# A hand-ordered attention and gated-MLP kernel on one core: new orders for all five engines, and a planner that counts instruction packets and load landings differently

## The chip, the cores and the metric

The kernel runs on one core of one Trainium2 chip. The time is that of one execution on the device, in microseconds. Three runs of the kernel before the change took 268.81, 270.65 and 270.70 us; their median is 270.65 us. One more execution, taken with the hardware profiler, took 270.25 us; its span, from the first instruction of the program to the last event that the profile sees, is 268.5 us. All durations below come from that one execution, and its time axis starts with the span.

## The reference, cut to what matters

S is 2048 tokens, D is 512, there are 32 heads of 16 elements, and the hidden size of the gated MLP is 1792. The 2048 tokens are cut into N = 4 segments of L = 512 tokens.

```python
x = A_x
g = sigmoid((x * gate_w).sum(-1, keepdims=True))
# part A: attention inside each segment, plus a memory of all segments before it
q, k, v = x @ wq, x @ wk, x @ wv            # per head, per segment of 512 tokens
for s in range(4):
    logits = qs @ ks.T * 0.25 + causal_mask
    a_dot  = softmax(logits) @ vs
    a_mem  = (phi(qs) @ M) / (phi(qs) @ z + 1e-6)    # phi(t) = t+1 if t>0 else exp(t)
    o      = sigmoid(beta) * a_mem + (1 - sigmoid(beta)) * a_dot
    M, z   = M + phi(ks).T @ vs, z + phi(ks).sum(0)
a = concat(o) @ wo
# part B
b = (gelu(x @ w_gate) * (x @ w_up)) @ w_down
out = g * a + (1 - g) * b
```

All inputs and the output are bfloat16; sums are kept in float32.

## The kernel before

**Tasks.** The work is cut into 1215 named tasks. A task runs on one engine and holds one or a few instructions. Names carry the segment first. `K1_2.0` and `K1_2.2` are the two halves (two matmuls each, over the four 128-row blocks of D) of tile 2 of K of segment 1; `Q`, `V`, `G` (gate), `U` (up) and `D` (down and wo) are named alike. `G1_10` is gate tile 10 of 14 for segment 1. In segment 0, K is cut into eight matmuls of 256 columns a tile (`K0_0.0` to `K0_0.7`), and Q goes to the four X banks. `warm0` to `warm10` multiply constants at the start, `x0t...` transpose x of segment 0 on TensorE and `x0ev...` copy it out. `Kn_tev`, `Qn_tev`, `Vevn_t` and `Gevn_t` copy a tile out of PSUM on ScalarE or VectorE; `Um` multiplies an up tile with the gelu of its gate tile; `kp`, `kl` write masked copies of K. `gmul`, `gsum`, `gexs`, `gts` make the output gate; `gmul0` needs `gate_w` broadcast (`w_gwb`).

**Attention.** For each group t of heads there are four or five rounds `qk s_t A0, B0, (L), A1, B1` (lines 849 to 905): matmuls into the four X banks, one exp on ScalarE over 2048 columns (L866), and a causal mask on GpSimd (L869). The next round must wait until exp has read the X banks. Between two rounds TensorE gets plain matmuls, mostly ten. `pv s_t_j` (L908, L916) multiplies the probabilities with V; `pvt` and `norm` follow on VectorE.

**Memory.** `pke s_i` (exp of K, ScalarE) and `pkc s_i` (three instructions on VectorE, L690, L692, L694) make phi(K) in place, i being the half of K's tiles. `pkT s_t` transposes tile t of it into `phkt` by DMA (L824, issued through L524). `mz s` (L828) multiplies it with V, and `num` reads the memory for the next segment. `xt s` later loads x into the same buffer `phkt`, and so waits for `mz` of the segment before. `Vlo s_j` (L744) copies half of V's rows into another layout, also by DMA, once all four V tiles are copied out.

**Loads.** wk and wq are issued by ScalarE's queue, everything else by SP's, in the order of SP's list, through `wdma` (L537) and `xdma` (L542), both over L528 or L524. The gate weights come in two halves: `w_wg0` holds tiles 0 to 6, `w_wg1` tiles 7 to 13 (L577). The up and down weights (`w_wu0`, `w_wu1`, `w_wd0`, `w_wd1`) come in halves too and are held back by reading a "tick" that an exp of segment 0 writes.

**What sets the order.** `ORDER` (line 36) is a list of task names for each engine, and each engine executes its list in that order. `schedule` (L235) doesn't choose an order. It walks the five lists with estimated durations and so fixes which of the four PSUM banks W a group of matmuls takes: the one that its estimates find free first. It also models DMA: a load lands at `dma_free`, which grows with the bytes and `DMA_RATE`. And it models the fetch of TensorE's instructions in blocks of `BLOCK`, each asked for when `BLOCK_ASK` instructions of it are done and needed at `BLOCK_END`. `Emitter.plan` and `finalize` then put a semaphore wait on every instruction whose operands another engine or a DMA writes, so the lists change what waits for what, not what is computed. SP also works strictly in its list's order: while it waits for one task's operands, no later load is issued.

```python
            best = None
            for e in ENGINES:
                t = queue[e][-1]          # the next task of this engine's list
                if npred[t.id]:
                    continue
...
            if t.nbytes:
                dma_free = max(t.finish + DMA_LAT, dma_free) + t.nbytes / DMA_RATE
                avail = dma_free
```

Of the kernel before, what the change touches and what calls it, by code (L numbers as in the profile page):

```python
# [7 lines left out]
PE, ACT, DVE, POOL, SP = "pe", "act", "dve", "pool", "sp"  # L8
# [26 lines left out]
BLOCK, BLOCK_ASK, BLOCK_END = 256, 165, 208  # L35
# [4 lines left out]
        "K0_1.4 K0_1.5 K0_1.6 K0_1.7 K0_0.4 K0_0.5 K0_0.6 K0_0.7 K0_3.3 K0_2.4 K0_2.5 K0_2.6 K0_3.4 K0_3.5 Q0_2.0 "  # L40
        "Q0_1.0 Q0_1.2 Q0_2.2 Q0_3.0 K0_2.7 Q0_3.2 K0_3.6 Q0_0.0 Q0_0.2 K0_3.7 V0_1.0 V0_1.2 V0_0.0 V0_0.2 "
        "qk0_0A0 G0_5.0 G0_5.2 V0_3.0 V0_2.0 V0_2.2 qk0_0B0 V0_3.2 Q1_3.0 Q1_3.2 G1_10.0 G1_10.2 qk0_0L G0_1.0 "
        "G0_1.2 G0_9.0 G0_9.2 G0_7.0 qk0_0A1 G1_9.0 Q1_0.0 G0_4.0 G1_9.2 G0_4.2 qk0_0B1 G0_7.2 G1_7.0 G1_7.2 "
        "Q1_0.2 G1_1.0 G1_1.2 qk0_1A0 G1_11.0 G1_5.0 G1_5.2 G1_11.2 Q1_1.0 qk0_1B0 G0_6.0 G1_2.0 Q1_1.2 G0_10.0 "
        "G1_2.2 qk0_1A1 G0_6.2 K1_2.0 G0_10.2 pv0_0_1 pv0_0_0 qk0_1B1 K1_2.2 K1_1.0 G1_8.0 Q1_2.0 Q1_2.2 qk0_2A0 "
        "G1_8.2 K1_1.2 G0_8.0 G0_8.2 G0_3.0 qk0_2B0 V1_2.0 G0_3.2 V1_2.2 pv0_1_1 pv0_1_0 qk0_2L mz0 V1_0.0 "
        "G0_13.0 V1_0.2 qk0_2A1 G0_13.2 V1_3.0 G1_12.0 V1_3.2 G0_2.0 qk0_2B1 G1_12.2 G1_0.0 G0_2.2 G1_0.2 G0_0.0 "
        "G0_0.2 qk0_3A0 K1_0.0 G1_6.0 G1_6.2 K1_0.2 G0_12.0 qk0_3B0 K1_3.0 G0_12.2 K1_3.2 Q2_2.0 Q2_2.2 qk0_3A1 "
        "G1_3.0 G1_3.2 G0_11.0 G0_11.2 pv0_2_1 pv0_2_0 qk0_3B1 V1_1.0 Q2_0.0 Q2_0.2 Q2_3.0 Q2_3.2 G1_13.0 V1_1.2 "
        "G1_4.0 G1_4.2 G1_13.2 U0_1.0 U0_1.2 U0_2.0 U0_4.0 U0_2.2 U0_9.0 U0_0.0 U0_4.2 U0_0.2 qk1_0A0 U0_9.2 "  # L50
        "U0_3.0 U0_3.2 U0_7.0 U0_7.2 U0_10.0 U0_8.0 U0_8.2 U0_13.0 U0_13.2 U1_0.0 U1_0.2 U0_5.0 U0_10.2 U0_5.2 "
        "U1_13.0 num1_00.0 U1_1.0 U1_1.2 U1_10.0 U1_13.2 U1_10.2 U0_6.0 U1_7.0 U0_6.2 U1_5.0 U1_7.2 U1_2.0 "
        "qk1_0B0 U1_5.2 U1_2.2 U1_11.0 pv0_3_0 pv0_3_1 qk1_0L U0_11.0 Q2_1.0 Q2_1.2 U1_3.0 U0_11.2 qk1_0A1 U1_3.2 "
        "D0_0.0 D0_0.2 num1_01.0 D0_0.4 U1_11.2 qk1_0B1 U0_12.0 num1_02.0 U0_12.2 D0_0.6 D0_0.8 D0_2.0 qk1_1A0 "
        "D0_0.10 U1_8.0 U1_6.0 U1_8.2 U1_6.2 D0_0.12 qk1_1B0 D0_0.14 D0_2.2 D0_0.16 D0_2.4 D0_2.6 qk1_1A1 D0_2.8 "
        "num1_12.0 num1_10.0 num1_11.0 D0_2.10 D0_2.12 D0_2.14 qk1_1B1 D0_2.16 U1_12.0 U1_9.0 U1_9.2 U1_12.2 "
        "qk1_2A0 pv1_0_0 pv1_0_1 pv1_1_1 mz1 pv1_1_0 qk1_2B0 D0_1.0 D0_1.2 D0_1.4 D0_1.6 D0_1.8 V2_3.0 qk1_2L "
        "D0_1.10 D0_1.12 D0_1.14 D0_1.16 V2_3.2 qk1_2A1 V2_0.0 D0_3.0 U1_4.0 K2_0.0 U1_4.2 qk1_2B1 V2_0.2 D0_3.2 "
        "K2_3.0 D0_3.4 K2_0.2 qk1_3A0 K2_3.2 K2_1.0 D0_3.6 K2_2.0 K2_1.2 qk1_3B0 K2_2.2 D0_3.8 V2_1.0 D0_3.10 "
        "D0_3.12 qk1_3A1 D0_3.14 D0_3.16 V2_1.2 Q3_1.0 Q3_1.2 G2_0.0 qk1_3B1 pv1_2_0 pv1_2_1 G2_0.2 G2_1.0 G2_3.0 "  # L60
        "G2_2.0 G2_3.2 G2_1.2 G2_2.2 G2_6.0 G2_6.2 G2_7.0 G2_4.0 G2_4.2 G2_5.0 G2_5.2 qk2_0A0 pv1_3_0 pv1_3_1 "
        "G2_7.2 G2_8.0 G2_10.0 G2_8.2 G2_10.2 G2_9.0 G2_9.2 G2_11.0 G2_12.0 G2_11.2 G2_12.2 G2_13.0 G2_13.2 "
        "U2_9.0 U2_9.2 num2_01.0 U2_8.0 U2_8.2 D1_0.0 D1_0.2 num2_00.0 D1_0.4 U2_13.0 U2_13.2 qk2_0B0 num2_02.0 "
# [36 lines left out]
    "dve": (  # L100
        "x0ev0a_0 x0ev0b_0 x0ev1_0 x0ev0_1 x0ev1_1 K0_1ev kl0_11 kp0_1 kl0_10 Q0_1ev K0_2ev kp0_2 Q0_0ev gmul0 "
        "gsum0_3 Vev0_0 Gev0_5 gsum0_0 kl0_31 kp0_0 gsum0_1 Q1_3ev Gev1_10 Vev0_3 gmat Gev0_9 pkc0_0 Gev1_9 kp0_3 "
        "Gev0_4 Gev1_7 Q1_0ev Gev0_7 Gev1_1 kl0_30 Gev1_5 Gev1_11 pkc0_1 Gev1_2 Gev0_6 Gev0_10 pvt0_0_1 pvt0_0_0 "
# [98 lines left out]
class Sched:  # L202
# [32 lines left out]
    def schedule(self):  # L235
# [8 lines left out]
        dma_free = 0.0  # L244
# [931 lines left out]
```

## Time and profile before

| what | value |
|---|---|
| median of three runs | 270.65 us |
| the profiled execution | 270.25 us |
| its span | 268.5 us |
| TensorE busy | 262.4 us (98%) |
| ScalarE busy | 210.5 us (78%) |
| VectorE busy | 202.2 us (75%) |
| GpSimd busy | 105.1 us (39%) |
| TensorE instruction packets (queue q8) | 23, 0.38 MB |
| granted TensorE clock | 1.00 |

In the lists of groups and in the timeline a line begins with start and length in microseconds (the timeline) or with the source line (the groups); then come engine, operation, output <- inputs, shapes and, after an x, how many alike were merged. `[0.44 <-DMA wq]` says that the engine was idle for 0.44 us just before, and that the DMA of wq ended it. PE is TensorE's matmul, PEld its weight load, DVE VectorE, ACT ScalarE, POOL GpSimd, SPq the DMA issues of SP's queue. A DMA line gives name, queue, count, size of one, and the median time from the beginning of its issue to its landing. The last matmul ends 2.9 us before the end of the span; the last copy and the last store to memory lie there.

### The profile page before, as it was taken

What the parts mean: (1) busy time and instruction counts of PE and PEld (TensorE: products, weight loads), DVE (VectorE), ACT (ScalarE), POOL (GpSimd) and SP (SyncE); (2) the same over time, 40 slices, a digit from 0 to 9 for tenths busy, and PEclk for the clock granted to TensorE, in tenths of its full rate; (3) what the DMA queues carried; (4) which work ended last, traced back from release to release, by engine and by line L of the source; (5) the groups of instructions that cost most, each with busy time, mean ns of one, the idle gap of its engine ahead of it and who ended that gap; (6) DMA issues with size and microseconds to landing.
All of it is one profiled execution on the core that took longest, in us unless ns stands there. A gap on an engine that the chain in (4) does not pass through costs nothing.

```text
span 268.5 us, 7155 instructions
## 1 busy us (share of the span) xinstructions
PE 262.4 (98%) x3021; PEld 119.2 (44%) x3021; DVE 202.2 (75%) x399; ACT 210.5 (78%) x180; POOL 105.1 (39%) x256
## 2 busy tenths in 40 slices
PE   8999999999999999899999999999999999999995
PEld 4543345334444435433444443543444444443452
DVE  1689989878988897868985877897691885685662
ACT  2689899989998987788868897779888768776801
POOL 8106582785200346161520628313771072326310
DMA  6950732892000055520000146230000002400002
GB/s 221 319 148 0 172 89 24 256 295 78 2 0 2 1 85 126 147 63 2 0 2 0 22 88 75 61 101 20 2 1 2 2 0 62 99 23 22 22 1 78
DMA packets 32752, 18.23 MB, mean 68 GB/s; under 512 B 20560, under 2 KB 32720, under 8 KB 32720
## 3 DMA queue, kind: packets, MB, share of 16 engines
q1 hardware_dynamic: 31632, 16.73, 25.6%
q10 hardware_dynamic: 1088, 1.05, 1.2%
q8 instruction: 23, 0.38, 0.6%
q14 instruction: 9, 0.07, 0.1%
HBM read 9.84 MB, written 2.10 MB: 44 GB/s over the span
## 4 chain that ended last, share of the span: by engine, by line
PE 90%; DMA 5%; SPq 2%; ACT 1%; issue 1%; ACTq 1%
PE psW L497 71%; PE psXALL L860 9%; PE psW L908 6%; DMA wq<-in_A_wq_dram 3%; PE psXALL L497 3%; DMA xT<-in_A_x_dram 2%; SPq L524 2%; PE psW L916 1%; ACT ptl L866 1%; ACTq L528 1%; PE psW L828 0%; SPq L528 0%; ACT ost L1036 0%; ACT hT L511 0%; ACTq L393 0%
## 5 line engine op out<-in xcount | busy, mean ns | idle before, releaser
L866 ACT ACTIVATE pt<-psXALL 128x2048 bf16<-128x2048 f32 x64 | 120.1, 1877 | 27.3 <-PE psXALL L860 24.5
L869 POOL TENSOR_SCALAR_AFFINE_SELECT pt<-pt 128x256 bf16<-128x256 bf16 x128 | 55.3, 443 | 111.9 <-ACT pt L866 107.0
L497 PE MATMUL psW<-xT,wu 128*128 128x512 bf16 x224 | 55.9, 380 | 0.0
L497 PE MATMUL psW<-wd,hT 128*128 128x512 bf16 x210 | 55.3, 380 | 0.0
L497 PE MATMUL psW<-xT,wg 128*128 128x512 bf16 x224 | 53.7, 380 | 0.0
L1007 DVE TENSOR_TENSOR hT<-psW,hT 128x512 bf16<-128x512 f32 x56 | 37.1, 684 | 19.1 <-PE psW L497 18.8
L869 POOL TENSOR_SCALAR_AFFINE_SELECT ptl<-ptl 128x512 bf16<-128x512 bf16 x32 | 23.9, 746 | 29.1 <-ACT ptl L866 27.4
L497 PEld LDWEIGHTS psW<-xT,wg 128*128 128x128 bf16 x224 | 20.6, 98 | 25.8 <-issue 1.9
L497 PEld LDWEIGHTS psW<-xT,wu 128*128 128x128 bf16 x224 | 20.7, 98 | 24.2 <-issue 1.7
L497 PEld LDWEIGHTS psW<-wd,hT 128*128 128x128 bf16 x210 | 18.4, 98 | 21.2 <-issue 2.7
L922 DVE STREAM_TRANSPOSE tb<-psW 128x512 f32<-128x512 f32 x32 | 21.7, 701 | 8.0 <-PE psW L916 7.7
L860 PE MATMUL psXALL<-qT,kpad 32*128 32x320 bf16 (+3 forms) x512 | 25.7, 273 | 1.3 <-issue 1.3
L860 PEld LDWEIGHTS psXALL<-qT,kpad 32*128 32x128 bf16 x512 | 7.7, 92 | 26.3 <-ACT pt L866 15.7
L908 PE MATMUL psW<-pt,vaug 128*17 128x192 bf16 (+3 forms) x512 | 18.8, 273 | 0.0
L991 ACT ACTIVATE hT<-psW 128x512 bf16<-128x512 f32 x28 | 15.3, 596 | 4.5 <-PE psW L497 4.5
L771 POOL COPY exsT<-exs 32x4 f32<-32x4 f32 x64 | 15.4, 240 | 8.2 <-ACT exs L762 4.6
L866 ACT ACTIVATE ptl<-psXALL 128x2048 bf16<-128x2048 f32 x8 | 15.0, 1877 | 4.5 <-PE psXALL L860 4.4
L497 PE MATMUL psW<-wv,xT 128*128 128x512 bf16 x64 | 18.1, 380 | 0.0
L497 PE MATMUL psW<-xT,wk 128*128 128x512 bf16 (+1 forms) x80 | 18.0, 337 | 0.0
L497 PE MATMUL psW<-wo,oT 128*128 128x512 bf16 x60 | 16.7, 379 | 0.1
L514 DVE CAST hT<-psW 128x512 bf16<-128x512 f32 x20 | 13.5, 686 | 4.3 <-PE psW L497 4.3
L908 PEld LDWEIGHTS psW<-pt,vaug 128*17 128x17 bf16 x512 | 10.4, 90 | 8.0 <-issue 3.0
(101 smaller groups left out, 310.7 us busy)
## 6 DMA issues: line engine op xcount, KB each, us to landing
out_dram<-ost SPq DMA_DIRECT2D x15, 128.0 KB, 2.0
wg<-in_B_w_gate_dram SPq DMA_DIRECT2D x2, 896.0 KB, 7.1
wu<-in_B_w_up_dram SPq DMA_DIRECT2D x2, 896.0 KB, 7.1
wd<-in_B_w_down_dram SPq DMA_DIRECT2D x2, 896.0 KB, 6.4
phkt<-in_A_x_dram SPq DMA_DIRECT2D x3, 512.0 KB, 5.1
vlow<-vaug SPq DMA_DIRECT2D x8, 136.0 KB, 2.7
wk<-in_A_wk_dram ACTq DMA_DIRECT2D x2, 256.0 KB, 4.6
hT<-in_A_x_dram SPq DMA_DIRECT2D x2, 256.0 KB, 4.2
```

Of the source, the lines that this page charges most:

```text
L497: return Instr(lambda e: e.matmul(view(), lhsT, rhs, start=first, stop=last), reads=reads, writes=[fkey if fkey is not None else g.key], e ...
L514: alts[DVE] = [Instr(lambda e: e.tensor_copy(dst(), src()), reads=reads, writes=writes, est=dve_t(n))]
L524: return e.dma_start_transpose(out_ap(), in_ap())
L528: return e.dma_start(out_ap(), in_ap())
L771: cross = task(f"exsT{s}", POOL, [Instr(lambda e, g=g, c=c: e.tensor_copy(exsT[sl][32 * g:32 * g + 32, c:16:4], exs[32 * c:32 * c + 32, s4 ...
L860: instrs.append(Instr(lambda e, g=g, lhs=lhs, rhs=rhs, c0=c0, ncol=ncol: e.matmul(X[g][:, c0:c0 + ncol], lhs(32 * g), rhs(32 * g), start=T ...
L866: exp_task(s, f"exp{s}_{t}{name}", [Instr(lambda e: e.activation(dst[:], XALL[:, :].rearrange("p (g c) -> p g c", g=4), ACTF.Exp, scale=AT ...
L869: task(f"msk{s}_{t}{name}", POOL, [Instr(lambda e, view=view, pat=pat, base=base: e.affine_select(out=view, in_=view, compare_op=ALU.is_ge ...
L908: instrs.append(Instr(lambda e, t=t, q=q, kb=kb, slot=slot, c0=c0: e.matmul(gp.f32()[32 * q:32 * q + 17, 128 * kb + 64:512], Vaug[sl][:, k ...
L922: task(f"pvt{s}_{t}_{j}", DVE, [Instr(lambda e: e.transpose(Tb[:, j, :], gp.f32()[:, :]), [gp.key], [("Tb", j)], dve_t(512))], grp=gp)
L991: lambda e, g=g, ft=ft, s=s: e.activation(hT[s % 2][:, ft, :], g.f32()[:, :], ACTF.Gelu_apprx_tanh),
L1007: task(f"Um{s}_{ft}", DVE, [Instr(lambda e, g=g, ft=ft: e.tensor_tensor(hT[sl][:, ft, :], g.f32()[:, :], hT[sl][:, ft, :], ALU.mult), [g.k ...
```

## The change

The five lists of `ORDER` are replaced by others. The planner's constants for the instruction fetch change; a table `LANDING` gives fixed landing times for the loads of the head, and in `schedule` a load that is in this table sets `dma_free` to its entry. Five byte counts in the planner are raised: xt from 524288 to 700000, wu and wd from 917504 to 1050000, wo from 524288 to 600000. No instruction is added or removed: each engine has the same tasks, except that some copies out of PSUM move between ScalarE and VectorE (three of the copies of x of segment 0 go from VectorE to ScalarE, all four `Vev0` now run on VectorE). The diff of the lists, cut to the places that are spoken of here:

```diff
-BLOCK, BLOCK_ASK, BLOCK_END = 256, 165, 208
+BLOCK, BLOCK_ASK, BLOCK_END = 254.4, 172, 192
+LANDING = {
+    "w_wk0": 4.8, "x0_0": 4.4, "w_wk1": 6.2, "x0_1": 5.8, "w_wq0": 8.2, "w_wv0": 7.4, "w_wq1": 10.1, "w_wv1": 8.9,
+    "w_wg0": 11.5, "x1_0": 12.1, "w_gwb": 12.4, "x1_1": 13.0, "w_beta": 13.3, "x1_2": 13.8, "x1_3": 14.3,
+    "w_wg1": 18.0,
+}
 ORDER = {
     "pe": (
...
-        "K0_1.4 K0_1.5 K0_1.6 K0_1.7 K0_0.4 K0_0.5 K0_0.6 K0_0.7 K0_3.3 K0_2.4 K0_2.5 K0_2.6 K0_3.4 K0_3.5 Q0_2.0 "
-        "Q0_1.0 Q0_1.2 Q0_2.2 Q0_3.0 K0_2.7 Q0_3.2 K0_3.6 Q0_0.0 Q0_0.2 K0_3.7 V0_1.0 V0_1.2 V0_0.0 V0_0.2 "
-        "qk0_0A0 G0_5.0 G0_5.2 V0_3.0 V0_2.0 V0_2.2 qk0_0B0 V0_3.2 Q1_3.0 Q1_3.2 G1_10.0 G1_10.2 qk0_0L G0_1.0 "
...
+        "K0_0.4 K0_0.5 K0_0.6 K0_3.3 K0_2.4 K0_0.7 K0_1.4 K0_3.4 K0_2.5 K0_2.6 K0_2.7 K0_1.5 K0_1.6 K0_1.7 K0_3.5 "
+        "Q0_0.0 Q0_1.0 K0_3.6 K0_3.7 Q0_0.2 Q0_1.2 Q0_2.0 Q0_3.0 Q0_3.2 Q0_2.2 V0_0.0 V0_0.2 V0_2.0 qk0_0A0 "
+        "V0_3.0 V0_1.0 V0_2.2 V0_3.2 V0_1.2 G0_5.0 qk0_0B0 G0_5.2 G0_1.0 G0_1.2 G1_5.0 G1_10.0 qk0_0L G1_10.2 "
...
-        "qk1_2A0 pv1_0_0 pv1_0_1 pv1_1_1 mz1 pv1_1_0 qk1_2B0 D0_1.0 D0_1.2 D0_1.4 D0_1.6 D0_1.8 V2_3.0 qk1_2L "
...
+        "D0_2.16 pv1_0_1 pv1_0_0 qk1_2A0 V2_3.0 D0_1.0 pv1_1_1 mz1 qk1_2B0 D0_1.2 D0_1.4 D0_1.6 D0_1.8 D0_1.10 "
+        "qk1_2L pv1_1_0 D0_1.12 D0_1.14 V2_3.2 U1_4.0 U1_4.2 qk1_2A1 D0_1.16 K2_3.0 D0_3.0 D0_3.2 D0_3.4 qk1_2B1 "
...
     "act": (
...
+        "w_wk0 w_wk1 w_wq0 w_wq1 tload x0ev0b_0 x0ev1_0 x0ev1_1 K0_0even K0_1ev K0_0ev pke0_0 Q0_1ev Q0_0ev "
+        "Q0_3ev Q0_2ev kl0_00 kl0_01 exp0_0A0 kl0_10 exp0_0B0 gsum0_3 exp0_0L gexp exp0_0A1 Gev1_9 exp0_0B1 "
...
     "dve": (
-        "x0ev0a_0 x0ev0b_0 x0ev1_0 x0ev0_1 x0ev1_1 K0_1ev kl0_11 kp0_1 kl0_10 Q0_1ev K0_2ev kp0_2 Q0_0ev gmul0 "
-        "gsum0_3 Vev0_0 Gev0_5 gsum0_0 kl0_31 kp0_0 gsum0_1 Q1_3ev Gev1_10 Vev0_3 gmat Gev0_9 pkc0_0 Gev1_9 kp0_3 "
...
+        "x0ev0a_0 x0ev0_1 K0_2ev kp0_2 kl0_11 K0_3ev kl0_30 gmul0 gsum0_2 kp0_1 kp0_0 kl0_20 Vev0_0 Vev0_2 Vev0_3 "
+        "Vev0_1 Gev0_5 Gev0_1 pkc0_0 kl0_31 Gev1_10 Gev0_9 Gev1_5 gmat gsum0_0 Q1_3ev Gev0_10 Q1_0ev gsum0_1 "
...
     "sp": (
-        "x0_0 x0_1 w_wv0 w_wv1 w_wg0 x1_0 w_gwb x1_1 w_beta x1_2 x1_3 w_wg1 pkT0_0 pkT0_1 Vlo0_0 Vlo0_1 w_wu0 "
-        "pkT0_3 pkT0_2 x2_3 xt1 w_wd0 w_wu1 x2_0 x2_2 x2_1 w_wd1 w_wo x3_1 oTd1_0 Vlo1_1 pkT1_0 Vlo1_0 oTd1_1 "
...
+        "x0_0 x0_1 w_wv0 w_wv1 w_wg0 x1_0 w_gwb x1_1 w_beta x1_2 x1_3 Vlo0_1 pkT0_1 w_wg1 Vlo0_0 pkT0_3 pkT0_2 "
+        "x2_3 pkT0_0 w_wd0 w_wu1 x2_1 x2_0 xt1 x2_2 w_wu0 w_wo Vlo1_1 w_wd1 oTd1_0 oTd1_1 pkT1_1 Vlo1_0 pkT1_0 "
...
@@ schedule @@
             if t.nbytes:
                 dma_free = max(t.finish + DMA_LAT, dma_free) + t.nbytes / DMA_RATE
+                if t.name in LANDING:
+                    dma_free = LANDING[t.name]
                 avail = dma_free
```

## The prediction

> **What bounds the kernel now.** I read the page's busy line first, then the chain of waits in order of time, then PE's timeline around each break of that chain, and last the timeline of the SP queue, the landing times of single DMAs and VectorE's timeline.
>
> ```profile
> PE 262.4 (98%) x3021; PEld 119.2 (44%) x3021; DVE 202.2 (75%) x399; ACT 210.5 (78%) x180; POOL 105.1 (39%) x256
> ...
> 10.50 1.47 PE L497 MATMUL psXALL<-xT,wq 128*128 128x512 bf16 x6 [0.44 <-DMA wq<-in_A_wq_dram]
> ...
> 57.52 0.38 PE L497 MATMUL psW<-xT,wq 128*128 128x512 bf16 x1
> 58.38 0.82 PE L497 MATMUL psW<-xT,wq 128*128 128x512 bf16 x3 [0.48 <-DMA xT<-in_A_x_dram]
> ...
> 108.83 0.31 PE L860 MATMUL psXALL<-qT,kpad 32*128 32x320 bf16 x3
> 110.42 0.39 PE L860 MATMUL psXALL<-qT,kpad 32*128 32x320 bf16 x5 [1.28 <-issue]
> ```
>
> TensorE is busy 98% of the span; no other engine is over 78%. So an order can gain only what TensorE loses in pauses, and a new pause costs its full length. A 512-column matmul starts 0.2165 us after the one before it (ten of them take 2.26 us in the chain, the last with a tail of about 0.16 us), so the pauses are read from starts. 57.52 to 58.38 is 0.86 instead of 0.22: 0.64 us lost on the landing of x of segment 2. 108.83 to 110.42 is 1.58 us lost ("issue": no semaphore is late; five attention and memory groups, 192 matmuls in 3.2 us, have outrun the instruction fetch). The same way, 0.60 us go before 10.50 (second half of wq), 0.31 us at 174.07 (six matmuls in 1.77 us instead of 1.46, after a like run of 192), and 0.20 us at 27.91. Together 3.3 us: that is all there is to win.
>
> **What the change takes away.** (1) Before the wq wait the new order puts all 32 K matmuls, where the old one had 29. Three more of 0.109 us are done by 10.49: -0.33 us; the rest of that wait stays. (2) In the old list w_wd0, w_wu1 and three x2 tiles stood behind xt1, which SP could issue only at 46.42, after mz0. In the new one w_wd0, w_wu1, x2_1 and x2_0 stand ahead of xt1 and can go from about 42, after exp0_2A0; xt1, x2_2 and w_wu0 follow mz0, which now comes at about 48.1. The old run moved 2.36 MB (xt1 and the two weight halves) from about 48.4 to 56.7, 0.284 MB/us; at that rate x2_2 has landed by about 54, and Q2_2.2 comes at 56.1: -0.64 us. w_wu0 then lands at about 57 and U0_1.0 comes at 59.1. (These times leave out any new pause, which would move both alike.) (3) The run pv1, pv1, pv1, mz1, pv1 is split: two groups, qk1_2A0 with two plain tasks, pv1_1_1 and mz1, then qk1_2B0 and ten plain matmuls, and only then pv1_1_0. 3021 matmuls were fetched in 23 instruction packets (the page's queue q8), 131 each. In the old trace the two dense runs went through 136 matmuls in 2.0 and 2.5 us and then paused; from 136 matmuls before the first stop (106.6) to the resumption at 110.42 it is 3.8 us, which I take as the time that a packet needs. Adding up the starts of the same kinds of matmuls in the new order, its densest 136 take 5.2 us: -1.58 and -0.31 us. (4) The 0.20 us at 27.91 goes, as that sequence is gone. Sum: **-3.1 us**, with 2.0 as the low end if one fetch or landing is late again. One more switch between plain and tiled matmuls (0.10 us in, 0.11 to 0.17 us out) adds **+0.2 us**. A lowered cost in the planner moves nothing by itself; only the four lists and the bank choices reach the chip.
>
> **What it moves that the timeline of SP prices.** In the SP list w_wg1, the second half of the gate weights, was directly behind x1_3; now it stands behind Vlo0_1 and pkT0_1.
>
> ```profile
> 5.09 0.57 SPq L528 DMA_DIRECT2D gwb<-in_gate_w_dram  x1
> ...
> 8.41 4.26 SPq L524 DMA_TRANSPOSE xT<-in_A_x_dram  x2
> 12.71 0.58 SPq L528 DMA_DIRECT2D wg<-in_B_w_gate_dram  x1
> 25.77 2.53 SPq L524 DMA_TRANSPOSE phkt<-kT  x2
> 28.42 1.36 SPq L528 DMA_DIRECT2D vlow<-vaug  x2
> 29.83 0.62 SPq L528 DMA_DIRECT2D wu<-in_B_w_up_dram  x1
> ```
>
> The reader is to see the gap from 12.71 to 25.77: SP issues in order, and the first phkt transpose had to wait for phi(K) on VectorE. w_wg1 was issued ahead of that gap; the new list puts it behind. Its landing in `LANDING` is a constant, 18.0, whatever the issue time.
>
> ```profile
> wg<-in_B_w_gate_dram SPq DMA_DIRECT2D x1, 896.0 KB, 5.2
> ...
> wu<-in_B_w_up_dram SPq DMA_DIRECT2D x1, 896.0 KB, 5.9
> ...
> gwb<-in_gate_w_dram SPq DMA_DIRECT2D x1, 128.0 KB, 7.7
> ...
> 23.32 0.59 DVE L690 TENSOR_SCALAR kT<-kT 128x1024 bf16<-128x1024 bf16 x1
> 23.83 0.87 DVE L692 TENSOR_SCALAR pex<-pex 128x1024 bf16<-128x1024 bf16 x1
> 24.73 1.01 DVE L694 TENSOR_TENSOR kT<-kT,pex 128x1024 bf16<-128x1024 bf16 x1
> ```
>
> When w_wg1 can be issued: in the new VectorE list pkc0_0 (the three rows above) stands behind gmul0, which needs gwb: 5.09 + 7.7 = 12.8. From there: gmul0 1.22, gsum0_2 0.65, three kp writes and kl0_20 about 0.9, four V copies at 0.61 from start to start, Gev0_5 0.61: 18.6. Gev0_1 waits for G0_1.2 on TensorE, done at about 19.3, and takes 0.65: 20.0. pkc0_0 took 2.42 us in the old trace and its sister pkc0_1 1.48: done at 21.5 to 22.4. Vlo0_1 has gone by then. pkT0_1 issues for 1.26 us (half of 2.53), so w_wg1 is issued at 22.8 to 23.7. The 896 KB landed 5.2 us after issue for wg and 5.9 for wu beside the V copies; here Vlo0_0 follows at once. So it lands at **27.9 to 29.6**, middle 28.7.
>
> When TensorE needs it: gate tile 10 is in that half, and G1_10.0 is the first to want it. In the new order, from the wq landing at 10.49 there are 38 plain matmuls (12 of Q, 16 of V, 10 of G) at 0.2165 and two qk groups at 0.43: 10.49 + 8.23 + 0.86 = **19.6**. The other guards on the way are met: the V copies free the banks from 17 on, Q's copies free X at about 14.0. The wait is 8.4 to 10.0 us, and I take **+9.2**. Behind G1_10.0 on TensorE stands everything, qk0_0L first, so ScalarE starves as well; SP, GpSimd and VectorE do not depend on it before pkT0_1, so it ends by itself. In the old order the same tile was asked for at 19.47 and had landed at 17.9: 1.6 us of slack were there. Nothing later gives the 9.2 us back, since TensorE has no idle time left to fill.
>
> What the pause does to the pace: in the old trace the 1.28 us pause at 109.14 was followed by matmuls at full pace: 0. The other row is the head, where a TensorE that had done nothing needs 4.07 us for ten warm-up matmuls (4,864 columns, 2.06 us at full pace, plus the tail): 1.8 us lost. A pause of nine microseconds is seven times the longest one seen, so I side with the head row: **+1.8**, with 0 as the other end. [...]
>
> **Sum.** The profiled run took 270.25 us for its span of 268.5; it lies 0.4 under the median of 270.65. 270.25 - 3.1 + 0.2 + 9.2 + 1.8 = **278.3 us**.
>
> **Rivals.**
> - The wait, without the slow pace (the 109.14 row holds for nine microseconds too): 276.5 us. Chance 0.14.
> - The wait and a second one: w_wu0 is now issued at about 51, last of the loads, and U0_1.0 comes at 59.1. One wu load landed in 5.9 us, but the median of the two is 7.1, so the other took 8.3; then U0_1.0 is up to 0.3 us late, and if a packet comes late as well, 1.58 stays: 278.3 + 1.9 = 280.2 us. Chance 0.13.
> - The other side, w_wg1 is not late. If SP reached it before 19.6 - 5.2 = 14.4 us, all pauses but half of the wq one would go and nothing come: 270.25 - 3.1 + 0.2 = 267.3 us, faster by over 1%. For it speaks that the old trace has SP free from 13.3 on; against it that pkT0_1 reads what pkc0_0 writes. It decides at one place, the end of pkc0_0. Chance 0.03.
> - The change does little: TensorE waits 3 us at most at G1_10.0 and stays at full pace, so gain and loss cancel: up to 270.4 us. That needs w_wg1 issued by 17.4, so pkc0_0 done by 16, ahead of the V copies that precede it. Chance 0.02.
> - The forecast: 0.68.
>
> **Numbers.** The range takes the low wait without the slow pace (270.25 - 2.9 + 8.4 = 275.8) and the long wait with one gain lost (270.25 - 1.8 + 10.0 + 1.8 = 280.3). The runs of before spread over 0.7%, so 1% is about what can be told from no change. Faster by over 1%: 0.03; within: 0.02; slower: 0.95.
>
> **What the new profile would show.** PE's timeline: one gap of 8 to 10 us before a matmul on wg at about 19.5, its releaser the DMA of wg, issued at about 23; then some 4 us in which 512-column matmuls start 0.43 apart. No "issue" gap near 100 to 110, no wait on xT near 60 to 70. The end is as now, with the last matmul 2.9 us before the end of the span. Wrong would be: wg issued before 15, or a gap that another tile had filled.

## The result, and the profile after

The changed kernel takes **283.29 us** (median of six runs), the kernel before 270.67 us (median of six runs beside them): a ratio of 1.0458, 95% interval 1.0404 to 1.0513. Medians here and below are of all executions, while ratios leave out those in a second, slower state (of the changed kernel's six one, 288.04 us; the other five have a median of 282.78). The forecast was 278.3 us with a range up to 280.3. The direction and the place of the main loss were right; the time lies 5.0 us above the forecast and 3.0 us above the range (4.5 and 2.5 by the median of the five). The profiled execution took 283.8 us (before: 270.25) for a span of 281.4 us (before: 268.5). What stood at L497 stands at L504 now, and all lines below it are 7 further down likewise; in some of the experiments they shift by one to three more, since a list is wrapped anew or a task is added.

The page's first two parts, engines and slices (PEclk is the granted TensorE clock in tenths, in 40 slices of 7.0 us):

```profile
PE 258.8 (92%) x2981; PEld 119.1 (42%) x3021; DVE 203.3 (72%) x400; ACT 208.0 (74%) x179; POOL 104.5 (37%) x256
...
PEclk9995799999999999999999999999999999999999
```

TensorE was busy 98% of the span and is busy 92%; the other engines do what they did. 40 of its 3021 matmul records are missing from this trace, so small gaps of 0.16 us in its timeline mean nothing; where small losses count, I add up the starts of the weight loads, which are all there. TensorE's timeline shows where the time went, in three breaks:

```profile
17.77 1.67 PE L504 MATMUL psW<-xT,wg 128*128 128x512 bf16 x7 [0.16 <-DVE vaug L521]
28.19 1.03 PE L504 MATMUL psW<-xT,wg 128*128 128x512 bf16 x2 [8.74 <-DMA wg<-in_B_w_gate_dram]
...
125.26 0.59 PE L504 MATMUL psW<-xT,wk 128*128 128x512 bf16 x2
129.30 1.04 PE L504 MATMUL psW<-wo,oT 128*128 128x512 bf16 x4 [3.44 <-DVE hT L1014]
...
187.35 0.29 PE L923 MATMUL psW<-ptl,vlow 128*17 128x64 bf16 x16
189.47 0.38 PE L504 MATMUL psW<-wv,xT 128*128 128x512 bf16 x1 [1.83 <-DVE tb L929]
```

The first break is the predicted one, in front of G1_10.0. The other two were not predicted: VectorE releases TensorE late in front of D0_3.0 (129.30) and V3_2.0 (189.47). The chain of waits tells why. Around the first break (start, length, what):

```profile
21.43 0.29 DVE klow L716
21.73 0.98 SPq L531
22.70 0.05 issue
22.75 5.40 DMA wg<-in_B_w_gate_dram
28.15 0.05 issue
28.19 1.03 PE psW L504 x2
```

SP issues the transpose pkT0_1 (L531) only when phi(K) is made, and w_wg1 behind it, at 22.75; it lands at 28.15. The chain names klow (kl0_31, the task behind pkc0_0) as what SP waited for, but SP's own row begins before klow has ended, 0.03 us after the last row of pkc0_0, and pkT0_1 reads what that row writes:

```profile
20.67 0.77 DVE L701 TENSOR_TENSOR kT<-kT,pex 128x1024 bf16<-128x1024 bf16 x1
21.46 1.24 SPq L531 DMA_TRANSPOSE phkt<-kT  x1
```

Around the two others, by the view of the chain again:

```profile
120.88 6.27 DMA phkt<-in_A_x_dram
127.15 0.02 issue
127.17 1.47 DVE phkt L758
128.64 0.61 DVE hT L1014
129.25 0.05 issue
129.30 1.47 PE psW L504 x6
...
181.10 6.22 DMA phkt<-in_A_x_dram
187.31 0.02 issue
187.34 1.23 DVE phkt L758
188.56 0.64 DVE tb L929
```

The DMA is xt2, x of segment 2 for the output gate; L758 is gmul2, which multiplies it with gate_w; L1014 is Um1_4, the product of up and gate that frees the PSUM bank that D0_3.0 wants. VectorE works in order, had been idle since 123.2 and could do nothing for 3.97 us, since gmul2 was its next task. At 187 the same happens with xt3, gmul3 and pvt2_0_1.

The balance, from the starts of the weight loads on TensorE: the last one starts at 265.17 us in the trace of before and at 278.0 now, 12.8 us later; what follows it takes 3.4 us in both. Counted by how much later a start comes than the median of its kind, the break at 28.19 with the slow pace after it takes 10.6 us, D0_3.0 3.6 and V3_2.0 1.7, together 15.9. Against that stand the pauses of before (wq, x of segment 2, the two that the prediction put down to the fetch, 27.91; 3.3 us together), which are gone.

### The profile page after: what moved, and what is told of

The parts are those of the page before. It is cut to its first block, busy times and chain, and to the rows that moved or that the text cites. A ratio compares the mean times of both kernels' runs of the same rounds, so it can differ in the third digit from the quotient of the medians.

```text
span 281.4 us, 7110 instructions
## 1 busy us (share of the span) xinstructions
PE 258.8 (92%) x2981; PEld 119.1 (42%) x3021; DVE 203.3 (72%) x400; ACT 208.0 (74%) x179; POOL 104.5 (37%) x256
## 3 DMA queue, kind: packets, MB, share of 16 engines
q1 hardware_dynamic: 31632, 16.73, 28.4%
## 4 chain that ended last, share of the span: by engine, by line
PE 86%; DMA 6%; ACT 2%; DVE 2%; issue 2%; SPq 1%; ACTq 0%
PE psW L504 66%; PE psXALL L867 8%; PE psW L915 5%; DMA phkt<-in_A_x_dram 4%; PE psXALL L504 3%; DMA wg<-in_B_w_gate_dram 2%; PE psW L589 1%; ACT pt L873 1%; PE psW L923 1%; DVE phkt L758 1%; SPq L531 1%; PE psW L835 1%; ACT ptl L873 1%; PE psXALL L598 0%; DVE kT L701 0%
## 5 line engine op out<-in xcount | busy, mean ns | idle before, releaser
L873 ACT ACTIVATE pt<-psXALL 128x2048 bf16<-128x2048 f32 x64 | 120.1, 1877 | 31.9 <-PE psXALL L867 28.9
L876 POOL TENSOR_SCALAR_AFFINE_SELECT pt<-pt 128x256 bf16<-128x256 bf16 x128 | 56.6, 452 | 131.5 <-ACT pt L873 126.7
L504 PE MATMUL psW<-xT,wg 128*128 128x512 bf16 x217 | 53.1, 386 | 9.5 <-DMA wg<-in_B_w_gate_dram 8.7
L504 PE MATMUL psW<-xT,wu 128*128 128x512 bf16 x217 | 54.9, 379 | 0.7 <-issue 0.5
L504 PE MATMUL psW<-wd,hT 128*128 128x512 bf16 x200 | 53.5, 380 | 0.8 <-issue 0.6
L1014 DVE TENSOR_TENSOR hT<-psW,hT 128x512 bf16<-128x512 f32 x56 | 37.1, 684 | 21.4 <-PE psW L504 20.2
L504 PEld LDWEIGHTS psW<-xT,wg 128*128 128x128 bf16 x224 | 21.1, 99 | 35.0 <-DMA wg<-in_B_w_gate_dram 9.2
L504 PEld LDWEIGHTS psW<-xT,wu 128*128 128x128 bf16 x224 | 20.9, 98 | 25.2 <-issue 1.7
L876 POOL TENSOR_SCALAR_AFFINE_SELECT ptl<-ptl 128x512 bf16<-128x512 bf16 x32 | 21.1, 661 | 27.0 <-ACT ptl L873 25.4
L504 PEld LDWEIGHTS psW<-wd,hT 128*128 128x128 bf16 x210 | 18.5, 98 | 21.5 <-issue 3.6
L873 ACT ACTIVATE ptl<-psXALL 128x2048 bf16<-128x2048 f32 x8 | 15.0, 1877 | 16.3 <-PE psXALL L867 15.9
L521 DVE CAST hT<-psW 128x512 bf16<-128x512 f32 x18 | 12.2, 685 | 11.7 <-PE psW L504 11.6
L504 PE MATMUL psW<-wo,oT 128*128 128x512 bf16 x56 | 15.4, 380 | 4.0 <-DVE hT L1014 3.4
L504 PE MATMUL psW<-wv,xT 128*128 128x512 bf16 x60 | 16.4, 380 | 2.3 <-DVE tb L929 1.8
L504 PE MATMUL psW<-xT,wk 128*128 128x512 bf16 (+1 forms) x75 | 16.4, 334 | 0.8 <-issue 0.8
L504 PE MATMUL psW<-xT,wq 128*128 128x512 bf16 x46 | 13.9, 387 | 0.3 <-issue 0.3
## 6 DMA issues: line engine op xcount, KB each, us to landing
out_dram<-ost SPq DMA_DIRECT2D x15, 128.0 KB, 1.7
```

The costliest lines, as they stand in the source:

```text
L504: return Instr(lambda e: e.matmul(view(), lhsT, rhs, start=first, stop=last), reads=reads, writes=[fkey if fkey is not None else g.key], e ...
L521: alts[DVE] = [Instr(lambda e: e.tensor_copy(dst(), src()), reads=reads, writes=writes, est=dve_t(n))]
L873: exp_task(s, f"exp{s}_{t}{name}", [Instr(lambda e: e.activation(dst[:], XALL[:, :].rearrange("p (g c) -> p g c", g=4), ACTF.Exp, scale=AT ...
L876: task(f"msk{s}_{t}{name}", POOL, [Instr(lambda e, view=view, pat=pat, base=base: e.affine_select(out=view, in_=view, compare_op=ALU.is_ge ...
L1014: task(f"Um{s}_{ft}", DVE, [Instr(lambda e, g=g, ft=ft: e.tensor_tensor(hT[sl][:, ft, :], g.f32()[:, :], hT[sl][:, ft, :], ALU.mult), [g.k ...
```

## The experiments

Theory: the time is 283.3 = (before, less some 3 of removed pauses) + 10.6 for w_wg1 with the slow clock + 5.3 for VectorE standing at gmul2 and gmul3 in front of work that TensorE waits for. Rivals: the slow clock costs nothing by itself; the new waits are not caused by the place of gmul2 or xt2 in the lists; the pause of 1.28 us in the kernel before doesn't come from the dense run of small matmuls.

### w_wg1 back in its place

```diff
 "sp":
-  x1_2 x1_3 Vlo0_1 pkT0_1 w_wg1 Vlo0_0
+  x1_2 x1_3 w_wg1 Vlo0_1 pkT0_1 Vlo0_0
```

> The changed kernel with one word moved: w_wg1 stands directly behind x1_3 in SP's list again, as in the kernel before. My theory: the wait of 8.7 us at G1_10.0 and the 1.8 us of half pace behind it go (10.6 us together from the starts of the weight loads), and nothing else changes: 283.3 - 10.6 = 272.7 us, ratio to before about 1.007; the gaps of 3.6 and 1.7 us that end with xt2 and xt3 stay. Rival one: those two gaps are after-effects of the late head, as they do not exist in the kernel before; then they go too: 267.4 us, ratio 0.988. Rival two: with w_wg1 in time another guard of the head (a bank held by a V copy) takes over part of the wait: 275 us or more.

Measured: 273.08 us, ratio 1.0075 (1.0051 to 1.0100), 10.2 us below the changed kernel. The wait at G1_10.0 and the slow pace after it are gone and TensorE stands at full clock through the head (1.00 in every window from 0 to 7 us and from 18 to 36 us). So one entry of SP's list is worth about 10 us; and without it the change still isn't faster than before, since the pause in front of D0_3.0 stays (3.07 us by the timeline's row, and 1.4 us more lost to a half clock behind it in this execution). The other pause, in front of V3_2.0, isn't there, though nothing in this edit concerns xt3: it landed 4.16 us after its issue here, 6.22 in the changed kernel's trace.

### gmul2 and gmul3 later on VectorE

```diff
 "dve":
-  pvt1_1_0 gmul2 Um1_4 gsum2_1 fin0_1 pqc2_1 K2_0ev K2_3ev gsum2_0
+  pvt1_1_0 Um1_4 fin0_1 pqc2_1 K2_0ev K2_3ev gmul2 gsum2_1 gsum2_0
...
-  Q3_2ev gmul3 pvt2_0_1 norm2_0 pvt2_1_1 pvt2_1_0 fin1_1
+  Q3_2ev pvt2_0_1 norm2_0 pvt2_1_1 pvt2_1_0 gmul3 fin1_1
```

> The changed kernel with w_wg1 still late, but gmul2 (and gsum2_1, which needs it) moved behind K2_3ev in VectorE's list and gmul3 behind pvt2_1_0. My theory: TensorE's gaps at 129 and 189 us come from VectorE standing at gmul2 and gmul3 for xt2 and xt3 while the copies behind them hold TensorE's banks; with these copies ahead the gaps of 3.6 and 1.7 us go: 283.3 - 5.3 = 278.0 us, ratio about 1.027. That is also what my prediction would have been right about without this term. Rival: the memory path itself (gate of segment 2, gexs2) is what is late; then the gaps only move and the time stays at 282 to 284 us.

Measured: 281.63 us, ratio 1.0398 (1.0361 to 1.0435), not the expected 278.0. The two breaks are gone as expected, but only 1.7 us of the 5.3 came out, and the interval still overlaps with that of the changed kernel. In its profile TensorE waits in two new places for an exp on ScalarE, 1.27 us at 135.26 and 1.54 us at 194.30. The next run, in which both this edit and the last one are made, shows why.

### Both

> Both edits: w_wg1 back behind x1_3, gmul2 and gmul3 later. My theory: the two causes are independent and add up: 283.3 - 10.6 - 5.3 = 267.4 us, ratio to before 0.988, so faster than both kernels, by the pauses that the old orders had. Rival: with the head in time, loads and VectorE work meet differently and new waits of 2 to 4 us appear: 269 to 272 us, ratio 0.995 to 1.005.

Measured: 271.51 us, ratio 1.0023 (0.9999 to 1.0048), not the expected 267.4 but where the rival had put it. TensorE waits in two other places. ScalarE's and then TensorE's timeline of this run:

```profile
117.68 1.88 ACT L873 ACTIVATE pt<-psXALL 128x2048 bf16<-128x2048 f32 x1 [0.71 <-PE psXALL L867]
121.14 0.63 ACT L763 ACTIVATE phkt<-phkt 128x512 bf16<-128x512 bf16 x1 [1.58 <-DVE phkt L758]
...
121.77 1.86 ACT L873 ACTIVATE pt<-psXALL 128x2048 bf16<-128x2048 f32 x1
```

```profile
123.68 0.40 PE L867 MATMUL psXALL<-qT,kpad 32*128 32x320 bf16 x8 [1.28 <-ACT pt L873]
```

The row at L763 is gsum2_3, which reads what gmul2 wrote. ScalarE works in order too: gsum2_3 now waits 1.58 us for the later gmul2, the exp behind it is late, and qk1_3B0 cannot have the X banks. The same happens one segment later with gsum3_0 (1.54 us at 182.72). The wait had moved from one engine's list to another's; I had priced the edit on VectorE alone. In the kernel before, gsum2_3 and gsum3_0 stood on VectorE: it isn't only copies out of PSUM that the change moves between ScalarE and VectorE, but `gsum`, `kl` and `fin` tasks too, and these two are what holds ScalarE here.

### TensorE kept busy during the wait

This kernel adds 128 matmuls of constants, 128 columns wide, to TensorE's list in front of G1_10.0; their product is not used. It adds work and takes nothing away.

```diff
+    gfill = Grp(banks)
+    task("fill0", PE, [Instr(lambda e: e.matmul(gfill.f32()[:, 0:128], ones[:, 0:128], ones[:, 0:128],
+                                                start=True, stop=True), [], [gfill.key], mm_t(128))
+                       for _ in range(128)], grp=gfill)
 "pe":
-  ... G1_5.0 G1_10.0
+  ... G1_5.0 fill0 G1_10.0
```

> The changed kernel, with 128 extra matmuls of constants (128 columns each, about 7.1 us, one instruction packet's worth) directly ahead of G1_10.0, so that TensorE works through most of its wait. Their results go to a PSUM bank that nobody reads. My theory: the wait for w_wg1 ends at the same time, about 28.2 us, but the granted clock stays full, and the 1.8 us of half pace are saved: 283.3 - 1.8 = 281.5 us, ratio about 1.040. Rival: half pace is covered by other waits behind it: no change, 283.3 us. Rival two: the extra matmuls delay the end of the wait: slower than 283.3 us.

Measured: 282.11 us, ratio 1.0429 (1.0397 to 1.0460), about 1 us below the changed kernel, with overlapping intervals, so the time alone decides nothing; the profile of this run is clear on the head. TensorE's timeline:

```profile
20.14 7.70 PE L592 MATMUL psW<-const-bfloat16-1.0 128*128 128x128 bf16 x128
29.25 0.38 PE L503 MATMUL psW<-xT,wg 128*128 128x512 bf16 x1 [1.42 <-DMA wg<-in_B_w_gate_dram]
```

The granted clock stays at 1.00 from 18 to 36 us, and after 29.25 matmuls start at full pace: four of 512 columns take 1.04 us at 29.91, where in the changed kernel four take 1.89 us at 29.71 under a clock of 0.50. So the slow pace in the changed kernel comes from the idle time and not from w_wg1 itself. Part of the gain was lost again because w_wg1 landed later in this execution (28.98 instead of 28.15), and part at D0_3.0: a pause of 2.45 us there was followed by 3.4 us of half clock in this execution, while the longer pause of the changed kernel (3.44 us) was not.

### w_wg1 halfway

```diff
 "sp":
-  x1_3 Vlo0_1 pkT0_1 w_wg1 Vlo0_0
+  x1_3 Vlo0_1 w_wg1 pkT0_1 Vlo0_0
```

> The changed kernel with w_wg1 between Vlo0_1 and pkT0_1 in SP's list: it no longer waits for pkc0_0, only for the V copies. My theory: the wait at G1_10.0 is set by the issue of w_wg1 and nothing else. SP is done with Vlo0_1 at 19.0 instead of issuing at 22.75, so w_wg1 lands 3.7 us earlier, at about 24.5, and the wait is about 5 us instead of 8.7. The granted clock fell 2.2 us after the last matmul in the changed kernel, so a wait of 5 us still brings half pace: 283.3 - 3.7 = 279.6 us, ratio about 1.032. Rival one: beside Vlo0_1 the load takes longer and the wait is hardly shorter: 282 us. Rival two: after 5 us the clock is still full: 277.8 us, ratio 1.026.

Measured: 278.19 us, ratio 1.0253 (1.0193 to 1.0314). w_wg1 goes out at 18.96, right behind Vlo0_1, and G1_10.0 starts at 24.04 after 4.66 us of waiting. The clock was at half from 21.5 to 28.4, so the rival on the clock falls. The time lies below the 279.6 expected, but the four executions spread from 275.7 to 283.4 us; in the profiled one, the shortest, xt2 landed in 3.8 us and D0_3.0 lost only 0.2 us. That made me doubt my own account of D0_3.0: perhaps it is no matter of order, but of a slow landing in some runs. The last four runs below are for that.

### The 1.28-us pause, alone, in the kernel before

```diff
 "pe":
-  pv1_0_0 pv1_0_1 pv1_1_1 mz1 pv1_1_0 qk1_2B0 D0_1.0 ... V2_3.0 qk1_2L
+  pv1_0_0 pv1_0_1 pv1_1_1 mz1 qk1_2B0 D0_1.0 ... V2_3.0 pv1_1_0 qk1_2L
```

> The kernel before with one task moved in TensorE's list: pv1_1_0 goes from behind mz1 to behind V2_3.0, so that eight qk matmuls and twelve plain ones stand between. It is one part of the change done alone. My theory: the 1.58 us pause (issue, at 110.4) is TensorE outrunning its instruction packets in a run of 192 short matmuls; with the run cut to 160 and slow matmuls behind it the packet is there in time, and the time falls by 1.1 to 1.6 us, to about 269.4 us, ratio 0.9945. Rival: the pause is the DMA queues being crowded at that moment; then it stays, wherever the run is cut: ratio 1.000.

Measured: 269.58 us, ratio 0.9967 (0.9945 to 0.9990): 0.9 us below the kernel before beside it (270.50), a little less than expected. In its profile the 1.28-us "issue" gap is gone. Its span is 266.7 against 268.5, but not all of that is the edit's: the waits for wq (0.60 us) and for x of segment 2 (0.64 us) and the 0.31 us at 174.07 are missing from this trace too, though the lists at those places are those of before. TensorE's timeline where it had been:

```profile
106.97 0.81 PE L827 MATMUL psW<-vaug,phkt 128*32 128x34 bf16 x64
108.19 0.40 PE L859 MATMUL psXALL<-qT,kpad 32*128 32x320 bf16 x8 [0.40 <-ACT pt L865]
108.52 1.04 PE L496 MATMUL psW<-wo,oT 128*128 128x512 bf16 x4
```

What is left ahead of the next round is 0.40 us that an exp ends. One group of 32 matmuls moved takes the pause away, in this profile and, by the interval, over the 12 executions; so the pause belongs to the order at that place, and the rival falls. But a dense run isn't enough for a pause: the other run of 192, from 169.2 to 172.2 us here, wasn't cut, and the six matmuls behind it take 1.49 us, at full pace, where they took 1.77. That it is the instruction fetch that runs out is argued, not shown: it is read from the absence of any semaphore in the gap.

### All waits followed through

Both edits of above; on ScalarE gsum2_3 moves behind exp1_3B0 and gsum3_0 behind exp2_2A1; on SP xt2 goes ahead of x3_3, and x3_1 behind pkT1_2.

```diff
 "act":
-  exp1_2B1 gsum2_3 exp1_3A0 K2_1ev exp1_3B0
+  exp1_2B1 exp1_3A0 K2_1ev exp1_3B0 gsum2_3
...
 "sp":
-  x3_1 pkT1_3 out0 pkT1_2 oTd1_3 oTd1_2 out2 x3_3 xt2 x3_2
+  pkT1_3 out0 pkT1_2 x3_1 oTd1_3 oTd1_2 out2 xt2 x3_3 x3_2
```

> The run with both edits, and the data of xt2 and xt3 asked for later or landed earlier everywhere: gsum2_3 goes behind exp1_3B0 and gsum3_0 behind exp2_2A1 in ScalarE's list (the run with both edits had 1.34 and 1.61 us of TensorE waiting for exps that stood behind them); xt2 goes ahead of x3_3 and x3_1 behind pkT1_2 in SP's list, so that out0 leaves earlier (0.8 us of waiting for the output buffer). My theory: each of these waits goes and nothing takes its place: 271.5 - 1.3 - 1.6 - 0.8 = 267.8 us, ratio 0.9885, faster than both kernels. Rival: the list's slack is used up and a new wait of 1 to 3 us appears: 269 to 271 us.

Measured: **268.60 us, ratio 0.9922** (0.9897 to 0.9947), faster than both kernels, though 0.8 us above the expected 267.8. One pause over 0.3 us is left, 0.40 at 125.84 behind a copy on VectorE.

### xt2 ahead of x3_3

The kernel with w_wg1 back in its place, and one more entry of SP's list:

```diff
 "sp":
-  oTd1_2 out2 x3_3 xt2 x3_2 x3_0
+  oTd1_2 out2 xt2 x3_3 x3_2 x3_0
```

> The run with w_wg1 back behind x1_3, and xt2 ahead of x3_3 in SP's list, nothing moved on VectorE. That run had a gap of 3.4 us that ends with xt2, and 1.2 us of half pace behind it. My theory: xt2 is late for two reasons, SP issues x3_3 (1.2 to 1.8 us) first and three x3 tiles share the queues; put first, it lands 2 to 3 us earlier, the gap is about 1 us, too short for half pace: 273.1 - 3.5 = 269.6 us, ratio 0.995. Rival: xt2 waits for mz1 and lands 6 us after its issue in any place: only the 1.2 us of the issue are won, 272 us.

Measured: 269.29 us, ratio 0.9945 (0.9911 to 0.9978), as expected; the profile has no pause at D0_3.0. The lists of VectorE and ScalarE are those of the changed kernel here: two entries of SP's list are enough to turn the 4.6% into a gain of 0.55%.

### Order or landing time: four kernels side by side

In the first four experiments xt2 landed 5.7 to 6.3 us after its issue, in the next four, on another chip, 3.8 to 4.6 us, whether it stood ahead of x3_3 or behind. To tell the order from the landing, the changed kernel, the same with xt2 first, the one with w_wg1 back, and the one with both ran together, on the chip of the first four.

> The changed kernel unaltered, beside the others. Theory: 1.045, with a pause over 3 us before D0_3.0 and xt2 landing 6.0 us or more after its issue. Rival (landing is a matter of the chip): on a chip where xt2 lands in about 4 us the pause shrinks to about 1.2 us and the ratio to about 1.037.

> The changed kernel with one entry of SP's list moved: the load of xt2 stands ahead of the transpose x3_3, so that it doesn't wait for mz1; w_wg1 stays late. My theory (xt2 comes late because its issue stands behind x3_3): xt2 goes out some 2 us earlier in its stretch, gmul2 starts within 1 us of VectorE being free, the 3.44-us pause before D0_3.0 goes, and the time is 3.4 to 3.7 below the changed kernel's on the same chip, about 279.7 us or 1.033 of the kernel before. Rival (how long xt2 takes to land is a matter of the chip: it took 6.0 to 6.3 us in the runs of one kind and 3.8 to 4.6 in others, whatever the order): the time here equals that of the changed kernel in these same runs.

> w_wg1 back behind x1_3 alone, beside the next kernel on the same chip. Theory: 1.007 to 1.008 of the kernel before, with the pause at gmul2 (xt2 behind x3_3). Rival (landing is a matter of the chip): if xt2 lands in about 4 us here, the pause is 1.5 us or less without any change of order, and the ratio is about 0.997.

> The kernel before this one with xt2 ahead of x3_3. Theory: 0.994 to 0.996 of the kernel before, 3.4 us or more below the run with xt2 behind x3_3 on this same chip. Rival (landing is a matter of the chip): the two differ by no more than 1.5 us.

| kernel | time | ratio to before (95%) | xt2 issued, landing after | pause before D0_3.0 |
|---|---|---|---|---|
| changed | 282.43 | 1.0448 (1.0388 to 1.0508) | 121.99, 5.8 us | 3.07 us |
| changed, xt2 first | 280.50 | 1.0360 (1.0293 to 1.0427) | 121.10, 3.8 us | none |
| w_wg1 back | 271.06 | 1.0039 (1.0007 to 1.0070) | 110.34, 5.0 us | 1.65 us |
| w_wg1 back, xt2 first | 268.68 | 0.9939 (0.9910 to 0.9968) | 109.55, 4.8 us | none |

The changed kernel came out as expected (1.0448, a pause of 3.07 us), though xt2 landed in 5.8 us and not in 6.0 or more. "w_wg1 back" (1.0039) lies between its theory (1.007) and its rival (0.997). The pair with w_wg1 back differs by 2.4 us, between the two expectations (3.4 and over, 1.5 and under): both have a part. The landing moves between 3.8 and 6.3 us over the executions, and the same kernel (w_wg1 back) took 273.08 us with a pause of 3.07 us at first and 271.06 us with one of 1.65 here.

What the order brings can be read off if the issue is counted from TensorE's own progress. On the time axis xt2 first goes out only 0.8 to 0.9 us earlier, but TensorE stood 0.9 and 1.0 us later in those two executions. K2_3.0 is the task directly ahead of D0_3.0 in all four kernels. xt2 goes out 4.34 us (changed) and 4.71 us (w_wg1 back) ahead of K2_3.0's start with x3_3 in front, and 6.22 and 6.42 us with xt2 first: the order brings 1.9 and 1.7 us. With w_wg1 back that is nearly all that D0_3.0 lost by the starts (1.8 us), for the landing is only 0.3 us shorter. In the changed kernel D0_3.0 had lost 3.2 us, and the landing, 2.0 us shorter, has the rest.

What sets the landing isn't settled: on the first chip it took 5.0 to 6.3 us behind x3_3, and 3.8 and 4.8 ahead of it; on the other 3.8 and 4.3 behind it, and 3.9 and 4.6 ahead of it; in the first profile of the kernel before 5.25. Whether the order also brings an earlier landing on the first chip can't be told from two executions. The load xt3, whose place none of the experiments touches, took from 4.2 to 6.2 us in these traces (4.2 to 5.6 on the first chip alone), so a landing can change by more than 1 us with neither the order around it nor the chip.

What stands ahead of xt2, in "w_wg1 back": first the row of x3_3 in SP's timeline, then the chain of waits.

```profile
108.36 1.81 SPq L531 DMA_TRANSPOSE xT<-in_A_x_dram  x1
```

```profile
107.79 0.69 PE psW L835 x64
108.48 0.33 PE psXALL L867 x8
108.81 0.55 PE psW L504 x2
109.36 0.81 SPq L531
...
110.34 5.04 DMA phkt<-in_A_x_dram
```

xt2 overwrites what mz1 (L835) reads, so it waits for mz1 in either place. mz1 ends at 108.48, and xt2 could go then: with xt2 first it goes out 0.15 us behind mz1's end in the kernel with w_wg1 back, here 1.86 us. In between SP is held by x3_3, for 1.81 us, where the two transposes before it took 2.57 together. The chain puts this down to two matmuls on TensorE (108.81). The kernel asks for no such wait: x3_3 overwrites x of segment 0, whose last reader on TensorE, U0_6.2, ran 19 us earlier. What makes the row longer is open. My expectation had xt2 held by mz1 only when it stands behind x3_3; that was wrong, and what it is held by there is the length of x3_3.

"Changed, xt2 first" gained 1.9 us and not 3.4 to 3.7: its profile has no pause at D0_3.0, but the half clock after the long wait lasted until 34.4 us instead of 32.8, which is 1.0 us of work lost, and mz1 waited 0.51 us for a transpose.

## Why the prediction was wrong, by its own steps

**What the change takes away, -3.1: right in the sum, shown in part.** All five pauses are gone in the new trace, and the run with one pv group moved takes the largest, 1.58 us, away by itself. But three of the other four (wq 0.60, x of segment 2 0.64, 174.07 0.31) are missing from that run's trace as well, with the lists of before at those places. They come and go between executions of one order, so that the new order removes them is not shown; of the wq wait the prediction had kept 0.27 us, and nothing in it foresaw that the rest goes too. Net of the late loads it is not all a gain, though: "w_wg1 is not late" was priced at 267.3 us, and the two kernels that make it so with xt2 in place took 268.7 and 269.3 us, with spans of 266.8 and 266.6, 1.7 to 1.9 below that of before. There D0_1.0 loses 1.1 us behind fin0_2 on ScalarE, which waits for the store out0. D0_1.0 now stands behind two pv groups, one round and V2_3.0, where it had stood behind all four pv groups, mz1 and a second round.

**w_wg1, +9.2: right.** Issue predicted 22.8 to 23.7, seen 22.75; landing 27.9 to 29.6, seen 28.15; G1_10.0 wanted at 19.6, seen at 19.3 (28.19 less the 8.9 us by which its start is late). The reason, too: pkT0_1 behind pkc0_0, whose last row ends at 21.43.

**The slow pace, +1.8: right.** The clock was at half until 31.9; half of the 3.7 us from 28.19 is 1.9 us. Both together: 11.0 predicted, 10.6 by the starts.

**The step that failed: the sum itself, which had no term for xt2 and xt3.** Under "what it moves that the timeline of SP prices" the prediction followed one load, w_wg1, and under (2) it followed xt1; it said that nothing later would give time back, and what might be added later it left to a rival, with 0.3 us at U0_1.0 and a late packet. It did not follow xt2 to gmul2, nor ask who stands behind gmul2 on VectorE. In both lists Um1_4 is the task behind gmul2. But in the old order of TensorE D0_3.0 stood ahead of U1_4, and the trace of before shows it at 116.82, ahead of gmul2 (117.49 to 118.67), so that it could not wait for Um1_4 (118.75):

```profile
110.78 0.45 SPq L528 DMA_DIRECT2D phkt<-in_A_x_dram  x1
...
116.82 0.59 PE L497 MATMUL psW<-wo,oT 128*128 128x512 bf16 x2
...
117.49 1.18 DVE L751 TENSOR_TENSOR phkt<-phkt,gwb 128x2048 bf16<-128x2048 bf16 x1
118.75 0.69 DVE L1007 TENSOR_TENSOR hT<-psW,hT 128x512 bf16<-128x512 f32 x1
```

In the new order D0_3.0 stands behind U1_4, and Um1_4 releases it. V3_2.0 moved likewise, from the last group of heads of its segment (behind qk2_3B0) to directly behind pv2_1_0.

What it would have come to with the landings of before: xt2 took 5.25 us to land there (110.78 to 116.03), gmul2 and Um1_4 another 1.87 (117.49 to 119.36). From the issue at 120.88 that gives 128.0 for D0_3.0, which was wanted at 125.86: 2.1 us. For xt3, 5.13 us there, and gmul3 and what follows it as in the new trace: 181.10 + 5.13 + 1.23 + 0.64 + 0.27 = 188.4 against 187.64: 0.7 us. So 2.8 us come from landings that the trace of before showed. The issue times and the times at which the two tasks were wanted are the new trace's; a forecast would have had to add them up from the lists, as the prediction did for w_wg1. Of the 5.3 us, the other 2.5 are, for the most part, landings of 6.27 and 6.22 us instead of 5.25 and 5.13 (2.1 us), and a gmul2 of 1.47 us instead of 1.18. With 2.8 the forecast would have been 281.1; the second run of the changed kernel took 282.4.

**The rival with a second wait (280.2) was right in kind.** It named U0_1.0 and a late packet. Neither is seen; the second wait stood at gmul2, and there was a third.

## What to carry to other kernels

When an engine's list is replaced, follow every load, not only the one that is plainly late: for each, its issue behind what stands ahead of it in its queue, its landing, the first task that reads it, and then whoever stands *behind* that task on the same in-order engine, up to TensorE. A task that reads a load is a gate in its engine's list, and moving it only helps if its readers on the other engines move as well: taken off VectorE's path, the same wait came back on ScalarE (1.58 us in front of gsum2_3). Where a landing time is a constant in a planner, move nothing past the load that it stands for without looking at its issue.

## What the runs showed of the hardware that was not expected

**Half clock lasted 3.4, 6.8 or 10.2 us.** The granted clock (the third column from the right in the table by windows: window, its length, busy time and count of each engine, then clock, DMA share and GB/s) of the changed kernel, of the one with xt2 first, and of "w_wg1 back" in its first run:

```profile
21.00:22.00 1.00, 0.00 (x0) 0.00 (x0) 0.71 (x2) 0.00 (x0) 0.00 (x0) 0.84 0.00 0
22.00:31.00 9.00, 2.81 (x38) 1.06 (x39) 0.22 (x1) 1.10 (x1) 0.00 (x0) 0.50 0.48 132
31.00:32.00 1.00, 1.00 (x4) 0.41 (x3) 0.47 (x1) 0.90 (x2) 0.15 (x1) 0.54 0.00 0
```

```profile
24.00:25.00 1.00, 0.00 (x0) 0.00 (x0) 0.00 (x0) 0.00 (x0) 0.00 (x0) 0.56 0.85 93
25.00:34.00 9.00, 5.80 (x44) 1.93 (x44) 0.69 (x1) 2.00 (x2) 1.97 (x3) 0.50 0.29 106
34.00:35.00 1.00, 1.00 (x12) 0.37 (x12) 0.80 (x2) 0.26 (x1) 0.66 (x1) 0.82 0.00 0
```

```profile
118.00:119.00 1.00, 0.00 (x0) 0.00 (x0) 1.00 (x2) 0.00 (x0) 1.00 (x1) 0.97 0.00 0
119.00:122.00 3.00, 2.51 (x6) 0.73 (x6) 2.97 (x6) 0.00 (x0) 1.30 (x4) 0.50 0.13 43
122.00:123.00 1.00, 1.00 (x11) 0.35 (x11) 0.08 (x1) 0.23 (x1) 0.00 (x0) 0.82 0.01 1
```

Taken as a mean of 1.00 and 0.50, a window at 0.84 was at half for 0.32 of its 1 us, one at 0.54 for 0.92. By this estimate the half clock lasted 0.32 + 9 + 0.92 = 10.24 us, 0.88 + 9 + 0.36 = 10.24 us, and 0.06 + 3 + 0.36 = 3.42 us; in four other runs it comes in the same way to 10.24 (the changed kernel again), 10.24 (gmul2 and gmul3 later), 6.84 (w_wg1 halfway) and 3.40 us (TensorE kept busy). The length of a pause of two to four microseconds did not decide whether half clock follows: it did after a pause of 2.45 us (TensorE kept busy), after one of 3.07 us in one run ("w_wg1 back") and not after one of the same length in another (the changed kernel again), and not after one of 3.44 us (the changed kernel at 129.30). What decides it, these runs do not show. After the long waits (4.66 to 8.87 us) the full clock came back 3.7 to 6.2 us after the first matmul.

**The first four microseconds run at half pace under a record of full clock.** TensorE's timeline of the changed kernel begins so:

```profile
0.84 4.06 PE L589 MATMUL psW<-const-bfloat16-1.0 128*128 128x512 bf16 x10 [0.84 <-PEq L1168]
```

4,864 columns would take 2.06 us at the later pace (0.2165 us for 512), plus a tail of 0.16; they take 4.06. The weight loads of the 512-column ones start 0.43 us apart, as they do at 30.11 to 31.39 under a clock of 0.50, while the table by windows gives a clock of 1.00 for every microsecond from 0 to 7. What slows them is not shown; in the head of this program the recorded clock does not tell the pace.
